# Moving the per-head finish of a cached attention kernel into the next loop turn, and building q and the MLP from wide matmuls

## The chip, the cores and the metric

The kernel runs on one core of one Trainium2 chip. The metric is the device time of one execution in microseconds (us). A run counts as slow if it is over 1.5% above the fastest run of the same kernel, and only fast runs are compared; all timed runs quoted here were fast, except one single look that is marked. "Granted clock" is the share of its full clock that the profile says PE was given in a stretch. The engines are PE (TensorE), VectorE (DVE in the profile), ScalarE (ACT), GpSimd (POOL) and SyncE (SP), which issues almost all DMA.

## The reference

It is one decode step. Attention A: 2 batches, 32 query heads on 8 key/value heads, 32,768 cached positions of width 128. MLP B works on the same input, and the result joins the two.

```python
xn = layernorm(x)                                  # [2,1,512]
q  = (xn @ wq)                                     # 32 heads of 128
p  = softmax(q . k_cache / sqrt(128)); o = p @ v_cache
s  = o.reshape(2, 1, 4096) @ wo
h  = gelu(layernorm(xn) @ w1); ...                 # shifted by 1 or 2 positions: all zero for S = 1
x1 = xn + hs                                       # = xn
g  = silu(x1 + gelu(layernorm(x1) @ w3) @ w4)
out = x + s * g
```

K and V are 134 MB each, so 268 of the 280.5 MB that the kernel reads are cache.

## The kernel before

There are 16 groups (batch, kv head). A group reads 8.4 MB of K and then 8.4 MB of V. All input but x (8 KB, on ScalarE's queue) goes through one SyncE queue in this order: wq, w3, w4, K0, V0, K1, V1, ... K15, V15, wo in eight parts.

```python
# SyncE: what each load waits for
load_k(0)                                # no wait
wait(sp, k_h2); load_v(0)                # the MLP's weights lie in V's buffer
for m in range(1, NG):
    sp.wait_ge(p_k, m); load_k(m)        # first half of group m-1's scores done
    sp.wait_ge(p_o, m); load_v(m)        # group m-1's V products done
for i, (g0, g1, c0, c1) in enumerate(WO_PARTS): ...   # wo parts: 2, 2, 1, 1, 1 kv heads, then 1/2, 1/4, 1/4 of one
```

```python
# PE: prologue (narrow matmuls, weights stationary)
for h in range(Hq):
    for k in range(DK):                  # q: 128 matmuls, 128x2
        pe.matmul(qT_ps[:, h*B:(h+1)*B], lhsT=wq3[:, k, h*Dh:(h+1)*Dh], rhs=xT[:, k, :], ...)
... # up projection 56 matmuls 128x2, down projection 56 matmuls 128x128
with pe.Fori(0, NG):                     # one group
    ... 64 score matmuls, sums, 64 V matmuls
    mm.then_inc(s_o, 1); mark(p_o)
    take(pe, s_ob)                       # the finish: head sums ...
    for t in range(VT): mm = pe.matmul(oT, lhsT=ob[:, t*Dh:(t+1)*Dh], rhs=sel_o[:, t, :], ...)
    mm.then_inc(s_x, 1)
    take(pe, s_on)                       # ... and head rows
    for r in range(NQ): mm = pe.matmul(xp[:, r, :], lhsT=sel_r[:, r, :, :]..., rhs=on[:, :], ...)
    mm.then_inc(s_x, 1)
pe.wait_ge(s_r, NG)                      # all 16 finishes done
for i, (g0, g1, c0, c1) in enumerate(WO_PARTS):
    wait(pe, (d_wo[i], 16)); ...         # 128 wo matmuls in all
```

The finish of a group is what turns its V products into normalized head outputs: ScalarE copies the products (`ob`), PE sums them (head sums) and lays them out (head rows), and VectorE does four short steps between and after. VectorE transposes K for the scores (16 instructions per group), then the exponentials, then its part of the finish (`rec`, `on`, `xm`, `oX`).

The softmax here doesn't subtract the row's maximum and nothing guards it: scores larger than these inputs give would overflow.

## Time and profile before

The time was 655.61 us (median of 3 runs, 655.14 to 656.74). The trace is of a run of 655.52 us, span 654.2 us.

| what | value | read from |
|---|---|---|
| DMA engines busy, rate | 99.2%, 429 GB/s | page |
| PE, VectorE busy | 62%, 52% | page |
| one group, K start to K start | 583.35 - 544.68 = 38.67 us | timeline |
| first V issued / first K block used | 29.58 / 42.53 us | timeline |
| last V half used / wo products / store issued | 641.25 / 648.43 to 651.75 / 652.46 us | timeline |

The page of before: its busy shares (part 1), the DMA row of the 40 slices (part 2), the main queue (part 3), and the chain that ended last (part 4).

```profile
PE 404.3 (62%) x2748; PEld 169.8 (26%) x2748; DVE 337.5 (52%) x429; ACT 71.4 (11%) x167; POOL 5.0 (1%) x18
...
DMA  8999999999999999999999999999999999999997
...
q1 hardware_dynamic: 6748, 280.50, 99.2%
...
PE 1%; DVE 0%; issue 0%; DVEq 0%
```

One resource is busy from end to end and the engines are not. The rate is 429 GB/s over the whole span and 433 from 80 to 649 us (windows view). Whether the engines could move more was not tested.

The timeline of before. The columns are start, duration, engine, line, operation, output and inputs, count, and in brackets the idle time before it with what ended it. First come the prologue's landmarks, then two starts of K transposes a group apart, then the tail.

```profile
18.44 3.57 PE L332 MATMUL bank<-xT,kbuf 128*128 128x2 bf16 x128 [2.09 <-DVE xT L325]
29.58 0.33 SPq L210 DMA_DIRECT2D vbuf<-in_A_v_cache_dram  x1
42.53 18.14 DVE L454 STREAM_TRANSPOSE T<-kbuf 128x1024 int32<-128x1024 int32 x16 [11.90 <-DVEq L46]
...
544.68 18.14 DVE L454 STREAM_TRANSPOSE T<-kbuf 128x1024 int32<-128x1024 int32 x16 [7.83 <-DVEq L46]
583.35 6.88 DVE L454 STREAM_TRANSPOSE T<-kbuf 128x1024 int32<-128x1024 int32 x6 [6.28 <-DVEq L46]
...
641.25 3.48 PE L515 MATMUL bank<-vbuf,pt 128*16 128x512 bf16 x32 [2.44 <-PEq L46]
648.43 3.32 PE L547 MATMUL bank<-kbuf,oX 128*17 128x128 bf16 x128 [0.79 <-DVE oX L472]
651.81 0.29 DVE L555 TENSOR_TENSOR sg<-bank,g 113x128 f32<-113x128 f32 x1 [3.43 <-PE bank L547]
```

VectorE sits idle for 11.9 us before the first K block and for several us in every group. At the end the 128 wo products start only after the last finish (`oX`), and they run in one piece.

### The profile page before, as it was taken

The page shows a single profiled execution, that of the slowest core. Times are in us where ns is not written, and L with a number is a line of the kernel's source. Part 1 is how long each engine was busy: PE and PEld are TensorE (multiplying, and loading weights), DVE is VectorE, ACT ScalarE, POOL GpSimd, SP SyncE. Part 2 cuts the span into 40 slices and gives each one's busy share as a digit, 9 for nine tenths or more (in the row PEclk, how much of TensorE's full clock was granted, in tenths as well). Part 3 has the DMA queues.
Part 4 walks back from the last instruction along what each step waited for, and adds up shares of the span by engine and source line. Part 5 has one row for each costly group of instructions (what it writes and reads, how often), then busy time and mean ns, then how long its engine had stood idle before and what let it go on. Part 6 is the DMA issues. An engine that isn't in the chain of part 4 may idle for free. (4 is left out here: it accounts for less than half of the span.)

```text
span 654.2 us, 7191 instructions
## 1 busy us (share of the span) xinstructions
PE 404.3 (62%) x2748; PEld 169.8 (26%) x2748; DVE 337.5 (52%) x429; ACT 71.4 (11%) x167; POOL 5.0 (1%) x18
## 2 busy tenths in 40 slices
PE   0538394583848558294764819468482956838785
PEld 0513132231323213132331313223131322313323
DVE  3238092653809256290835619074470916538560
ACT  1200102001010201101020010200101020010100
POOL 2000000000000000000000000000000000000000
PEclk9999789685977869697795969877597877869886
DMA  8999999999999999999999999999999999999997
GB/s 369 438 442 445 442 429 421 437 445 445 405 441 441 449 401 449 437 445 421 429 441 441 445 405 445 437 449 409 441 437 445 445 405 441 441 449 393 449 417 298
DMA packets 6766, 280.59 MB, mean 429 GB/s; under 512 B 736, under 2 KB 1000, under 8 KB 2024
## 3 DMA queue, kind: packets, MB, share of 16 engines
q1 hardware_dynamic: 6748, 280.50, 99.2%
q8 instruction: 4, 0.07, 0.0%
q14 instruction: 2, 0.02, 0.0%
q10 hardware_dynamic: 12, 0.01, 0.0%
HBM read 280.50 MB, written 0.00 MB: 429 GB/s over the span
## 5 line engine op out<-in xcount | busy, mean ns | idle before, releaser
L497 PE MATMUL bank<-T,z 128*128 128x512 bf16 x1024 | 282.1, 424 | 168.4 <-PEq L46 163.6
L454 DVE STREAM_TRANSPOSE T<-kbuf 128x1024 int32<-128x1024 int32 x256 | 290.8, 1207 | 129.2 <-DVEq L46 129.1
L497 PEld LDWEIGHTS bank<-T,z 128*128 128x128 bf16 x1024 | 97.5, 103 | 338.9 <-issue 261.6
L515 PE MATMUL bank<-vbuf,pt 128*16 128x512 bf16 x1024 | 77.3, 469 | 2.4 <-PEq L46 2.4
L467 DVE RECIPROCAL rec<-bank 128x4 f32<-128x4 f32 x16 | 2.9, 183 | 124.1 <-DVEq L46 124.1
L433 ACT ACTIVATE ep<-bank 128x512 bf16<-128x512 f32 x32 | 19.1, 597 | 438.2 <-ACTq L46 438.2
L515 PEld LDWEIGHTS bank<-vbuf,pt 128*16 128x16 bf16 x1024 | 28.2, 105 | 43.4 <-issue 28.1
L461 DVE STREAM_TRANSPOSE pt<-ep 128x512 bf16<-128x512 bf16 x32 | 22.1, 691 | 23.4 <-DVEq L46 23.4
L508 PE MATMUL bank<-sm,ones_f 128*128 128x4 f32 x64 | 10.5, 270 | 29.3 <-PEq L46 29.3
L526 PE MATMUL bank<-sel_o,ob 128*128 128x4 f32 x128 | 16.4, 252 | 13.8 <-PEq L46 13.8
L437 ACT COPY ob<-bank 128x512 f32<-128x512 f32 x16 | 9.4, 586 | 109.1 <-ACTq L46 109.1
L426 ACT ACT_TABLE_LOAD x16 | 20.5, 1283 | 0.3
L526 PEld LDWEIGHTS bank<-sel_o,ob 128*128 128x128 f32 x128 | 15.5, 191 | 18.3 <-issue 18.3
L508 PEld LDWEIGHTS bank<-sm,ones_f 128*128 128x128 f32 x64 | 9.6, 215 | 30.2 <-issue 30.2
L426 ACT COPY z<-qr 32x16 bf16 x64 | 12.9, 201 | 0.7
L532 PE MATMUL bank<-on,sel_r 128*128 128x4 bf16 x64 | 3.9, 165 | 12.6 <-PEq L46 12.6
L295 PE MATMUL bank<-ident,xn_bf 17*128 17x17 bf16 x4 | 0.3, 177 | 13.7 <-POOL x L286 13.7
L484 PE MATMUL bank<-ident 128*1 128x1 bf16 x64 | 8.3, 165 | 0.0
L484 PEld LDWEIGHTS bank<-ident 128*1 128x1 bf16 x64 | 4.0, 82 | 16.2 <-issue 14.5
L470 DVE TENSOR_TENSOR xm<-bank,mask 128x16 f32<-128x16 f32 x16 | 2.8, 175 | 8.6 <-DVEq L46 8.6
L532 PEld LDWEIGHTS bank<-on,sel_r 128*128 128x128 bf16 x64 | 2.9, 98 | 13.5 <-issue 13.5
L433 ACT ACTIVATION_READ_ACCUMULATOR ep<-bank 128x1 f32 x32 | 6.3, 198 | 0.2
(67 smaller groups left out, 58.2 us busy)
## 6 DMA issues: line engine op xcount, KB each, us to landing
kbuf<-in_A_k_cache_dram SPq DMA_DIRECT2D x2, 4096.0 KB, 22.1
vbuf<-in_A_v_cache_dram SPq DMA_DIRECT2D x2, 4096.0 KB, 27.2
kbuf<-in_A_wq_dram SPq DMA_DIRECT2D x1, 4096.0 KB, 12.2
vbuf<-in_B_w_dram SPq DMA_DIRECT2D x2, 1792.0 KB, 17.2
kbuf<-in_A_wo_dram SPq DMA_DIRECT2D x2, 1024.0 KB, 34.9
kbuf<-in_A_wo_dram SPq DMA_DIRECT2D x3, 512.0 KB, 37.3
kbuf<-in_A_wo_dram SPq DMA_DIRECT2D x1, 256.0 KB, 26.4
kbuf<-in_A_wo_dram SPq DMA_DIRECT2D x2, 128.0 KB, 15.6
```

The source lines that it names most:

```text
L426: i = act.copy(out=z[32 * j:32 * j + 32, :, :, c:c + rep], in_=qr[32 * j:32 * j + 32, :, :, bass.ds(m * rep, rep)],)
L433: act.activation(out=eps_[i][:, :], in_=sc[i][:, :], func=ACT.Exp, scale=inv_sqrt_dh, accum_out=rss[i][:, :]).then_inc(s_e, 1)
L437: act.copy(out=ob[:, :], in_=o[:, :]).then_inc(s_ob, 1)
L454: dve.transpose(out=Ts[(NR * i + r) % T_BUFS][:, :].rearrange("p (b t k) -> p t b k", b=NB, t=RT), in_=kt[:, r * W:(r + 1) * W].rearrange( ...
L461: dve.transpose(out=pts[h][:, :, :].rearrange("p r (t h) -> p t r h", h=rep), in_=eps_[i][:, :].rearrange("p (t r h) -> p t r h", r=NR, h= ...
L467: then(dve.reciprocal(out=rec[:, :], in_=S))
L484: pe.matmul(mark_ps, lhsT=ident[:, 0:1], rhs=ident[:, 0:1], start=True, stop=True).then_inc(sem, 1)
L497: mm = pe.matmul(sc[i][:, :], lhsT=z[:, nb, e, zc:zc + 128], rhs=Tb[:, nb, :, e], start=(r == 0 and nb == 0 and e == 0), stop=(r == NR - 1 ...
L508: pe.matmul(S, lhsT=ones_f[:, :], rhs=sms[h][:, :], start=(h == 0), stop=(h == NPART - 1))
L515: mm = pe.matmul(o[32 * j:32 * j + VT * rep, :], lhsT=pts[h][:, r, a * VT * rep:(a + 1) * VT * rep], rhs=vt[:, u * VT:(u + 1) * VT, :].rea ...
L526: mm = pe.matmul(oT, lhsT=ob[:, t * Dh:(t + 1) * Dh], rhs=sel_o[:, t, :], start=(t == 0), stop=(t == VT - 1))
L532: mm = pe.matmul(xp[:, r, :], lhsT=sel_r[:, r, :, :].rearrange("p j w -> p (j w)"), rhs=on[:, :], start=True, stop=True,)
```

## The change: intent and diff

The finish of a group moves to the start of the next turn. The last group's finish is left over, and is placed between the wo parts, so that products of heads that are already done need not wait for it. In the prologue, activations become the stationary operand (`lhsT`) and weights the moving one (`rhs`; 128x512 where before has 128x2): 62 wide matmuls on column tiles (each writes 32 of the 128 output partitions, four side by side) replace 240 narrow ones. VectorE transposes put the results back, and ScalarE and GpSimd spread q over the partition groups with 16 copies.

```diff
 # prologue
-    for h in range(Hq):
-        for k in range(DK):
-            i = pe.matmul(qT_ps[:, h * B:(h + 1) * B], lhsT=wq3[:, k, h * Dh:(h + 1) * Dh], rhs=xT[:, k, :], ...)
+    for t in range(NQB):
+        for k in range(DK):
+            for n in range(NQ):
+                i = pe.matmul(sc[t][32 * n:32 * n + 32, :], lhsT=xT[:, k, :],
+                    rhs=wq3[:, k, c:c + GW].rearrange("p (h w e) -> p h e w", h=rep * NB, e=2),
+                    ..., tile_position=(0, 32 * n))
+    for t in range(NQB):
+        k_qT = V(dve.transpose(out=qT[:, :, t * 16:(t + 1) * 16].rearrange("p r k -> p k r"), in_=sc[t]...))
+    for n in range(NQ):
+        for j in range(NQ):
+            if n < 2 or j < 2: k_qa = A(spread(act, j, n))
+            else:              k_qg = G(spread(pool, j, n))
 ... (cut: the two MLP products in the same style; four matmuls that gather the second)
 # loop
 with pe.Fori(0, NG):
+    head_sums()
+    head_rows()
     take(pe, s_z)
 ...
-    take(pe, s_ob) ... head sums ... take(pe, s_on) ... head rows
 # VectorE, in the same way: heads(...) before group(...), once more after the loop
 # tail
-pe.wait_ge(s_r, NG)
-for i, ... in enumerate(WO_PARTS): ...
+pe.wait_ge(s_r, NG)                      # the dummy finish of the first turn makes this "15 groups done"
+product(0)
+head_sums()
+product(1)
+head_rows()
+for i in range(2, len(WO_PARTS)):
+    if WO_PARTS[i][1] == Hkv and WO_PARTS[i - 1][1] < Hkv:
+        pe.wait_ge(s_r, NG + 1)
+    mm = product(i)
```

## The prediction

> **What bounds the kernel now.** The input stream. The page shows the 16 DMA engines 99.2% busy on one queue over the span of 654.2 us: 280.5 MB, 429 GB/s; PE 62%, VectorE 52%. The windows view gives 439 GB/s from 3 to 41 us and 433 from 80 to 649. [...] By the timeline one group takes 38.7 us (K transposes start at 544.7 and 583.4): 16.8 MB at 434 GB/s. Only three places could give time: the queue running dry at the start or in the loop, and the work after the last byte.
>
> **Start.** q, MLP and z setup are done at 32.5 us (timeline), but VectorE gets its first K block only at 42.5. The one load that depends on the prologue, the first V, is issued at 29.6, 12 us before the queue would need it. The change replaces 240 narrow matmuls (q 3.6 us, MLP up 3.5, down 1.7) by 62 wide ones on column tiles, plus 4 fp32 selections. The V products, same 128x512 form on column tiles, run 64 in 3.6 us, so I estimate 2 us for q and under 1 us for each MLP product. VectorE loses about 2 us of selector copies and gains three transposes of 0.5-0.7 us (estimate from 0.69 us for 128x512 bf16). ScalarE gets 12 and GpSimd 4 spreading copies, 0.2-0.3 us each. I expect the first V issue 2 to 4 us earlier, z ready at 27 to 33 us. All of it hides under the K load: worth 0.
>
> **Loop.** The order per engine is the same in a rotated loop: the finish still comes between V products and the next K transposes. The marks that release loads stay. K is issued about 8 us, V about 10 us before the queue runs out. Worth 0.
>
> **End.** The last V half arrives at 641.2; its products end at 644.6, then ob copy, head sums, VectorE, head rows, final oX at 648.4. Only then do 128 wo products run without a wait, 648.43 to 651.79 at a granted clock of 0.5; then two VectorE steps of 0.3 us and the store. But the wo parts are still landing: by issue plus landing time, parts 4 to 7 land at 649.9, 650.5, 650.8 and 651.16. After the change parts 0 to 3 run while PE waited, and behind the last landing only part 7's 4 matmuls remain (26 ns each, plus 0.3 us for one to drain). Their end moves from 651.79 to about 651.5: worth 0.3 us, at most 0.6.
>
> **Prediction: 655.3 us, 654.4 to 656.6.** Faster by over 2%: 0.01; within 2%: 0.98; slower: 0.01.
>
> **What would show it right.** DMA share still 99% at 429-430 GB/s; group period still 38.7 us; first K transpose still at 42.5 us though PE's prologue is shorter; wo products in pieces with PE waiting for landings, the last within 0.2 us of the last landing; the chain of waits ending in a DMA landing rather than the oX reduction.
>
> **What would make it wrong.** The first K transpose or the last landing moving by over 1 us: then the stream depends on something in the prologue that I took to be hidden. Spreading copies or strided and fp32 matmuls so slow that the first V issue passes 42 us would cost the excess.

The sum comes to 655.61 less 0.3 for the end and 0 for start and loop: 655.3 us. Of the terms behind the 0.3 us, 26 ns is 3.35 us / 128, and "0.3 us for one to drain" is the 311 ns that one of these products takes in the trace of before (median; the granted clock was 0.50 up to 651.3 us). The 0.2 to 0.3 us of a spreading copy was an estimate; small copies take 0.21 us on ScalarE (`z`) and 0.28 us on GpSimd (17x128) in that trace.

## The result, and the profile after

The changed kernel takes 655.26 us (median of 6 runs, 655.17 to 655.64), and before in the same comparison 655.21 us (6 runs, 655.12 to 656.74). The ratio is 0.9997, 95% interval 0.9984 to 1.001: the same. (A ratio is the mean time of one kernel's fast runs over that of the other's fast runs of the same rounds, so it is not quite the ratio of the medians quoted.)

The page of after, the same parts as shown of before (its DMA row of the slices is the same, digit for digit):

```profile
PE 403.5 (62%) x2586; PEld 163.9 (25%) x2586; DVE 339.4 (52%) x425; ACT 75.0 (11%) x179; POOL 6.6 (1%) x24
...
q1 hardware_dynamic: 6748, 280.50, 99.3%
...
DMA 4%; SPq 2%; PE 1%; issue 0%; DVE 0%
```

The DMA share is the same, and the chain that ended last now runs back into a DMA rather than into the finish.

The timeline of after, the same landmarks:

```profile
17.35 3.61 PE L347 MATMUL bank<-kbuf,xT 128*32 128x512 bf16 x32 [1.14 <-DVE xT L332]
19.30 1.09 DVE L356 STREAM_TRANSPOSE qT<-bank 128x512 f32<-128x512 f32 x1 [2.00 <-PE bank L347]
22.10 3.86 ACT L363 CAST qr<-qT 32x64 bf16<-32x64 f32 x12 [7.48 <-DVE qT L356]
27.28 0.23 ACT L409 ACTIVATE th<-inner 128x28 f32<-128x28 f32 x1
29.92 0.33 SPq L208 DMA_DIRECT2D vbuf<-in_A_v_cache_dram  x1
...
544.49 18.14 DVE L488 STREAM_TRANSPOSE T<-kbuf 128x1024 int32<-128x1024 int32 x16 [9.30 <-DVEq L46]
583.17 3.50 DVE L488 STREAM_TRANSPOSE T<-kbuf 128x1024 int32<-128x1024 int32 x3 [9.52 <-DVEq L46]
...
641.07 1.90 PE L570 MATMUL bank<-vbuf,pt 128*16 128x512 bf16 x32 [1.53 <-PEq L46]
...
648.44 0.61 PE L590 MATMUL bank<-kbuf,oX 128*17 128x128 bf16 x16 [0.59 <-DMA kbuf<-in_A_wo_dram]
649.69 0.60 PE L590 MATMUL bank<-kbuf,oX 128*17 128x128 bf16 x16 [0.64 <-DMA kbuf<-in_A_wo_dram]
650.48 0.83 PE L590 MATMUL bank<-kbuf,oX 128*17 128x128 bf16 x16 [0.19 <-DMA kbuf<-in_A_wo_dram]
651.37 0.29 DVE L608 TENSOR_TENSOR sg<-bank,g 113x128 f32<-113x128 f32 x1 [3.63 <-PE bank L590]
```

Three readings follow.

- Loop: the period is 583.17 - 544.49 = 38.68 us, against 38.67.
- Start: the first V is issued at 29.92 us, 0.3 us later than before, although far fewer matmuls run. The spreading copies stand in front of `tanh` (`th`) on ScalarE.
- End: the wo products come in six pieces, and five of them wait for a DMA landing (the last three are shown). The last four products start at 651.03 us, 0.04 us after the last landing. The step after them starts at 651.37 instead of 651.81.

Part of those 0.44 us is not the change. The last input packet ends at 650.88 us in the trace of before and at 650.70 in that of after. From that packet to the first packet of the store it takes 2.87 us before and 2.60 us after. So the new end is 0.27 us shorter in this pair of traces, and the rest is where the stream happened to end. The times of before scatter by more than that. And the pair differs in one more thing: the last 32 V products took 3.48 us in before, at a granted clock of 0.53, and 1.90 us in after, at 1.00. The next section sets the 0.27 us against this.

### The profile page after: what moved, and what is told of

Its sections match the earlier page's. It is cut to its first block, busy times and chain, and to the rows that moved or that the text cites. A ratio compares the mean times of both kernels' runs of the same rounds, so it can differ in the third digit from the quotient of the medians.

```text
span 653.8 us, 6890 instructions
## 1 busy us (share of the span) xinstructions
PE 403.5 (62%) x2586; PEld 163.9 (25%) x2586; DVE 339.4 (52%) x425; ACT 75.0 (11%) x179; POOL 6.6 (1%) x24
## 5 line engine op out<-in xcount | busy, mean ns | idle before, releaser
L570 PE MATMUL bank<-vbuf,pt 128*16 128x512 bf16 x1024 | 74.7, 457 | 1.5 <-PEq L46 1.5
L570 PEld LDWEIGHTS bank<-vbuf,pt 128*16 128x16 bf16 x1024 | 28.0, 103 | 40.5 <-issue 23.5
L525 PE MATMUL bank<-sel_o,ob 128*128 128x4 f32 x136 | 18.3, 258 | 14.4 <-PEq L46 14.4
L525 PEld LDWEIGHTS bank<-sel_o,ob 128*128 128x128 f32 x136 | 17.3, 199 | 19.0 <-issue 18.9
L533 PE MATMUL bank<-on,sel_r 128*128 128x4 bf16 x68 | 5.6, 165 | 12.8 <-PEq L46 12.6
```

Of the source, the lines that this page charges most:

```text
L525: mm = pe.matmul(oT, lhsT=ob[:, t * Dh:(t + 1) * Dh], rhs=sel_o[:, t, :], start=(t == 0), stop=(t == VT - 1))
L533: mm = pe.matmul(xp[:, r, :], lhsT=sel_r[:, r, :, :].rearrange("p j w -> p (j w)"), rhs=on[:, :], start=True, stop=True,)
L570: mm = pe.matmul(o[32 * j:32 * j + VT * rep, :], lhsT=pts[h][:, r, a * VT * rep:(a + 1) * VT * rep], rhs=vt[:, u * VT:(u + 1) * VT, :].rea ...
```

## The experiments

The theory is that the input stream sets the time. Then the prologue and the finish are hidden under it, and only work after the last landing (the moment when all data of a load are there) can be saved, which is about 0.3 us. The main rivals are two. First, a gain at the end is real and larger, and the new prologue eats it. Second, the loop is bound by a chain of engines that includes the finish, and the DMA share only follows.

### The two halves alone, and the copies out of the way

`end_only` is the kernel before with the new order of finish and wo. `start_only` is the changed kernel with the old order. `spread_late` is the changed kernel with one block moved:

```diff
 # spread_late: ScalarE and GpSimd copies behind tanh and sigmoid
-    wait(act, k_qT); wait(pool, k_qT); for n ...: for j ...: spread(...)     # in front of the MLP
     ... MLP, tanh, sigmoid ...
+    wait(act, k_qT); wait(pool, k_qT); for n ...: for j ...: spread(...)
```

> The kernel before with only the new order of the finish and the wo parts; prologue untouched. Theory (the input stream binds, and only the work after the last landing can be saved): 0.2 to 0.5 us less than before, wo products in pieces, the last one starting within 0.2 us of the last wo landing, loop period unchanged at 38.7 us. Rival 1 (the finish is on the critical path of the tail for its full length): 4 to 7 us less. Rival 2 (moving the finish in the loop delays K or V issues enough to drain the queue): slower by 1 us or more with a longer group period.

> The changed kernel with the old order of the finish and of wo; only the new prologue differs from before. Theory: within 0.3 us of before, first V issue at about 29.9 us, first K transpose at about 42.4 us, 128 wo products in one block that ends at about 651.8. Rival (the new prologue costs something that cancels a gain at the end): 0.3 us or more slower than before.

> The changed kernel with its 16 spreading copies moved behind tanh and sigmoid on ScalarE's queue. My prediction had the first V issue 2 to 4 us earlier than before, the trace has it 0.3 us later. If the copies in front of tanh (3.9 us on ScalarE) are the reason, the first V issue comes at about 26.4 us, 3 to 4 us earlier than in the changed kernel. If they are not, it stays near 29.9. Time in either case within 0.3 us of the changed kernel (about 655.2), because the first V issue is 12 us ahead of need.

Five runs of each were timed, and before had 655.54 us (9 runs, 655.28 to 656.75).

| kernel | median us (range) | ratio to before (95%) | last input packet to first store packet |
|---|---|---|---|
| end_only | 655.32 (654.89 to 655.53) | 0.9993 (0.9979 to 1.0007) | 2.60 us |
| start_only | 655.44 (655.36 to 656.85) | 1.0000 (0.9986 to 1.0014) | 2.74 us |
| spread_late | 655.25 (654.94 to 655.28) | 0.9991 (0.9977 to 1.0004) | 2.61 us |

No ratio is clear of 1, so the measured times do not prove a gain of 0.3 us. The rival with 4 to 7 us is refuted, and a prologue that eats a gain is not seen (one of a few tenths of a us could not be).

The last column is read from the DMA packets of one trace each. With the new order it is 2.60 or 2.61 in all four traces there are (after, end_only, spread_late and contig, a run below). With the old order it is not fixed: 2.87 and 2.74 here, but 2.60 in act_9, 2.54 in v_less, 3.42 in q_x7 and 4.11 in q_x4, runs of later sections that keep the old end. It goes with the time of the last 32 V products: 1.90 us at a granted clock of 1.00 in act_9 and v_less, 3.1 to 3.6 us at 0.50 to 0.59 in the other four. The tail of act_9 shows the old order with fast V products; the last of its wo products wait for a landing, too:

```profile
643.89 1.90 PE L525 MATMUL bank<-vbuf,pt 128*16 128x512 bf16 x32 [1.81 <-PEq L46]
652.50 1.63 PE L557 MATMUL bank<-kbuf,oX 128*17 128x128 bf16 x32 [0.26 <-DMA kbuf<-in_A_wo_dram]
```

With the new order the last V products took 1.90 us (after, spread_late), 2.95 (end_only) or 3.39 (contig), and the tail stayed the same. So the new end has no fixed worth of 0.27 us. It is worth nothing where the last V products had a granted clock of 1.00 (act_9, v_less), and 0.1 to 0.3 us in the traces of before and start_only (for the longer tails of q_x7 and q_x4 there is no counterpart with the new order). No run set the clock, so this is read across traces and not shown by an experiment. One more observation, not tested: none of the 16 timed runs of after, end_only and spread_late is above 655.64 us, while every list of before (6 to 9 runs) has one to three above 656.3, and start_only has one at 656.85. None of these was traced; a longer tail at the lower clock, as in q_x4, could be the reason.

In spread_late the first V issue moved as it should if the copies delayed it. The timeline of spread_late:

```profile
23.69 0.23 ACT L401 ACTIVATE th<-inner 128x28 f32<-128x28 f32 x1 [7.62 <-DVE inner L399]
25.88 0.33 SPq L208 DMA_DIRECT2D vbuf<-in_A_v_cache_dram  x1
```

It is issued at 25.88 instead of 29.92 us, and the time did not follow. The 12 copies on ScalarE (3.86 us in a row) were the reason for the late issue, together with a load of an activation table (`ACT_TABLE_LOAD`, 1.28 us) that in the changed kernel comes between the last copy and `tanh`; in spread_late it is not on that path.

### Fewer bytes, same compute

```diff
 def load_v(m):                                   # v_less: the kernel before
-    load(A_v_cache, vbuf[:, :], s_v, m)
+    if 0 < m < last:                             # seven eighths of V, the rest keeps old data
+        w = slice(0, 7 * SLOT // 4)
+        sp.dma_start(out=vbuf[:, w], in_=row_view(A_v_cache, *groups[m])[:, w]).then_inc(s_v[0], 16)
+        sp.sem_inc(s_v[1], 16)
+    else:
+        load(A_v_cache, vbuf[:, :], s_v, m)
```

> The kernel before, where groups 1 to 14 load only seven eighths of their V block (the rest keeps older data, so the result is wrong on purpose); all compute stays. 14.7 MB fewer at 433.7 GB/s. Theory (stream binds in the loop): 33 to 34.5 us faster, about 621.4, group period about 36.3 us. Rival (a chain of PE, VectorE and ScalarE binds the loop and the DMA share of 99% only follows it): 0 to 5 us.

It took 621.47 us (4 runs, 621.34 to 621.84) against 655.50, so 34.0 us less, with a group period of 551.90 - 515.64 = 36.26 us:

```profile
515.64 18.14 DVE L459 STREAM_TRANSPOSE T<-kbuf 128x1024 int32<-128x1024 int32 x16 [6.99 <-DVEq L46]
551.90 1.25 DVE L459 STREAM_TRANSPOSE T<-kbuf 128x1024 int32<-128x1024 int32 x1 [5.52 <-DVEq L46]
```

The 14.68 MB left out, at 433 GB/s, are 33.9 us. All instructions of the loop still ran. A group of 15.73 MB in 36.26 us is 434 GB/s, as in before (16.78 MB in 38.67 us). Bytes are what the loop costs. (Its output is wrong, which doesn't matter for the time. The comparison with the reference passed all the same, presumably because attention adds little to this output. It would not notice such an error.)

### How much slack the loop has

Idle copies on ScalarE in front of the second exponential delay the V products, the finish and the next V issue in every group.

```diff
 for i in range(NPART):                           # ScalarE loop of the kernel before
     take(act, s_sc)
+    idle(8 * i)                                  # loop_6;  idle(18 * i) in loop_12
     act.activation(out=eps_[i][:, :], in_=sc[i][:, :], func=ACT.Exp, ...)
+# idle(n): n times act.copy(junk1 <- junk0, 128x512 fp32), each followed by a wait for itself
```

> The kernel before with 8 idle copies (5 to 6.5 us) on ScalarE in every group in front of the second exponential, so that V products, finish and the next V issue come that much later. Read from before: K start to K start takes at least 29.2 us by compute (583.35 to 612.56, where K lay ready) against 38.7 us by the stream, so about 9.5 us of slack. Theory: group period unchanged at 38.7 us, only the last group is exposed at its end by at most a few us, so 0 to 3 us slower in all. Rival (the compute chain with the finish is what sets the period): 5 to 6.5 us per group, 80 to 100 us slower.

> The same with 18 idle copies (11 to 14.5 us per group), more than the slack of 9.5 us. Theory: the queue now runs dry in every group; period 40.5 to 45 us, 30 to 95 us slower, with gaps in the stream. If it is again within 3 us of before, the slack is larger than I read it.

loop_6 took 668.18 us (4 runs, 665.16 to 669.47) and loop_12 took 767.10 us (766.88 to 768.20), against 655.42. The timelines of loop_6 and of loop_12, each with two successive groups:

```profile
546.51 18.14 DVE L464 STREAM_TRANSPOSE T<-kbuf 128x1024 int32<-128x1024 int32 x16 [0.60 <-DVEq L46]
585.17 5.75 DVE L464 STREAM_TRANSPOSE T<-kbuf 128x1024 int32<-128x1024 int32 x5 [1.19 <-DVEq L46]
```

```profile
627.54 18.14 DVE L464 STREAM_TRANSPOSE T<-kbuf 128x1024 int32<-128x1024 int32 x16
672.38 3.50 DVE L464 STREAM_TRANSPOSE T<-kbuf 128x1024 int32<-128x1024 int32 x3 [0.50 <-DVEq L46]
```

With 8 copies (5.7 us) the period stays at 38.66 us: VectorE's idle time before K shrinks from 6 to 8 us to about 1, and the queue stays full. With 18 copies (13.15 us) the period is 44.84 us here, 44.2 to 45.9 in others, and the DMA packets show gaps of 4.3 to 6.5 us in every group. So the slack lies between 5.7 and 13.2 us. I had read 9.5; the delay minus the longer period, 13.15 - 6.2, gives about 7. The finish has room for several us per group in the loop, and shortening it there gains nothing.

My expectation of at most 3 us for loop_6 missed the end. In its profiled run (665.16 us, the fastest of the four; what the median has on top, 3.0 us, was not traced) the stream ends 1.8 us later than before, and 7.8 us more come after the last input packet (10.68 us to the store instead of 2.87). The last group has no next load to hide under. Its delay came out in full, plus the wo products that then had to wait for it. My 30 to 95 us for loop_12 missed in the same way: it was 111.7 us slower. The last input packet came 93.6 us later, but the tail behind it took 21.03 us instead of 2.87.

### Which end of the stream hides the finish

The eight wo parts are queued ahead of the last V block instead of behind it, once in each kernel:

```diff
     sp.wait_ge(p_o, m)
+    if m == last:
+        for i, (g0, g1, c0, c1) in enumerate(WO_PARTS): d_wo[i].after(sp.dma_start(...), 16)
     load_v(m)
-for i, (g0, g1, c0, c1) in enumerate(WO_PARTS): d_wo[i].after(sp.dma_start(...), 16)
```

> The kernel before, with the wo parts queued ahead of the last V block instead of behind it; nothing else changes. Now the stream ends with V, so the last products, the finish and the 128 wo products all lie behind the last landing: read from the trace of before, landing at about 651.0 plus 3.4 products, 3.8 finish, 3.4 wo, in all about 10.6 us, where before has 0.6. Theory (wo landing last is what hides the finish): about 10 us slower than before, 665. Rival (the finish is not hidden by the wo landing): within 2 us of before.

> The changed kernel with the same move of the wo parts. Theory: here the interleaving of finish and wo parts is on the critical path, and is worth 1.5 to 3 us: about 662 to 663.5, against about 665 of the same move on the kernel before. Rival (interleaving has no value of its own): no difference between the two.

The kernel before with this move took 665.95 us (4 runs, 665.28 to 666.98), and the changed kernel with it 662.46 us (662.26 to 662.96). Unmoved, before had 655.76 in the same rounds (655.09 to 656.75). The timelines of the two tails, first of wo_first_before, then of wo_first_after:

```profile
651.41 3.59 PE L516 MATMUL bank<-vbuf,pt 128*16 128x512 bf16 x32 [6.03 <-PEq L46]
659.52 3.60 PE L548 MATMUL bank<-kbuf,oX 128*17 128x128 bf16 x128 [0.79 <-DVE oX L473]
663.17 0.29 DVE L556 TENSOR_TENSOR sg<-bank,g 113x128 f32<-113x128 f32 x1 [3.70 <-PE bank L548]
```

```profile
651.33 3.59 PE L571 MATMUL bank<-vbuf,pt 128*16 128x512 bf16 x32 [6.04 <-PEq L46]
654.71 1.07 PE L591 MATMUL bank<-kbuf,oX 128*17 128x128 bf16 x32
657.00 0.63 PE L591 MATMUL bank<-kbuf,oX 128*17 128x128 bf16 x32
658.02 1.17 PE L591 MATMUL bank<-kbuf,oX 128*17 128x128 bf16 x64
659.24 0.29 DVE L609 TENSOR_TENSOR sg<-bank,g 113x128 f32<-113x128 f32 x1 [0.51 <-PE bank L591]
```

With the tail exposed, the interleaving is worth 665.95 - 662.46 = 3.5 us; I had expected 1.5 to 3. Some of that may be clock: the windows view grants 0.50 during the wo products of the first trace and 0.82 in the second, and the head sums between took 1.84 and 1.28 us. Whether the busier PE brought the clock about is not shown. With wo landing last, the interleaving is worth at most 0.3 us in the traces of before and after. This is where most of the possible gain went: before the change, the landing of wo already hid the finish and most of the wo products.

### How much slack the prologue has

Two kernels repeat the q matmuls of before (the result stays right), and a third delays `tanh` by idle copies:

```diff
-for h in range(Hq):
+for h in list(range(Hq)) * 4:                    # q_x4;  * 7 in q_x7
     for k in range(DK): pe.matmul(qT_ps[:, h*B:(h+1)*B], ...)
 # act_9
+idle(12)                                         # ScalarE, in front of tanh
 k = A(act.activation(out=th[:, :], in_=inner[:, :], func=ACT.Tanh, scale=GELU_C))
```

> The kernel before with its 128 q matmuls done four times (three of them redundant, same result): 3 times 3.5 us more prologue. The first V issue moves from 29.6 to about 40.1 us; the data queued ahead of it end at 41.84. Theory (prologue hidden under the first K load): 0 to 0.5 us slower. Rival (prologue exposed one for one): 10.5 us slower, about 666.

> The kernel before with its q matmuls done seven times: 6 times 3.5 us more, first V issue at about 50.6 us. Theory: the slack of about 12 us is used up and the queue stands empty from 41.8 to about 51.6 us (issue plus 1 us to the first packet), so 9 to 10.5 us slower, about 665. Rival (prologue exposed one for one): 21 us slower, about 676. Rival (prologue never matters): 0.

> The kernel before with 12 idle copies (128x512 fp32, about 0.6 to 0.8 us each with the wait between them) on ScalarE in front of tanh: the first V issue goes from 29.6 to about 37 to 39 us, without more code for PE (the redundant q matmuls of the two earlier runs turned out to stall PE 3.5 us per 128, so those runs overshot the slack). The data queued ahead end at 41.85. Theory (12 us of slack in front of the first V issue): 0 to 0.4 us slower, no gap in the stream. Rival (prologue exposed one for one): 7 to 10 us slower.

The "1 us to the first packet" of q_x7 agrees with the first load in the trace of before: issued at 0.73, first packet at 1.76 us. The 0.6 to 0.8 us of an idle copy was an estimate: one ScalarE copy of 128x512 fp32 takes 0.59 us in that trace, and the twelve with their waits then took 8.72 us in act_9.

| kernel | first V issued at, us | median us (range) | before, same rounds | ratio (95%) |
|---|---|---|---|---|
| act_9 | 39.65 | 658.17 (657.82 to 658.47) | 655.42 | 1.004 (1.0023 to 1.0056) |
| q_x4 | 51.37 | 667.95 (666.09 to 669.98) | 655.50 | 1.0181 (1.0163 to 1.02) |
| q_x7 | 61.55 | 679.19 (677.58 to 679.62) | 655.50 | 1.0354 (1.0337 to 1.0371) |

All three of my expectations failed here, for two reasons. I had expected at most 0.4, 0.5 and 10.5 us more; it was 2.75, 12.45 and 23.69.

The first is the size of the delay. Three more passes of q moved the V issue by 21.8 us, not by 10.5. The timeline of q_x4, PE only, shows why, and one line of q_x7 shows when it stops:

```profile
18.44 5.81 PE L332 MATMUL bank<-xT,kbuf 128*128 128x2 bf16 x212 [2.09 <-DVE xT L325]
28.18 3.55 PE L332 MATMUL bank<-xT,kbuf 128*128 128x2 bf16 x128 [3.93 <-issue]
35.48 3.55 PE L332 MATMUL bank<-xT,kbuf 128*128 128x2 bf16 x128 [3.75 <-issue]
42.50 1.31 PE L332 MATMUL bank<-xT,kbuf 128*128 128x2 bf16 x44 [3.47 <-issue]
```

```profile
42.31 11.68 PE L332 MATMUL bank<-xT,kbuf 128*128 128x2 bf16 x428 [3.20 <-issue]
```

PE pauses for 3.5 to 3.9 us per 128 matmuls, and nothing in the program makes it wait. In the DMA records a packet of 16,384 bytes on the instruction queue starts at 25.76, 33.17 and 40.26 us, and each time PE resumes 2.2 to 2.4 us later. In q_x7 the data queue is empty from 41.85 us; the instruction packets then come every 3.5 us, and 428 matmuls run without a pause. I read this as PE waiting for its instructions (128 matmuls and 128 weight loads per pause) while the data stream kept the DMA engines full. That is inferred from these times; no run tested it.

The second is the slack itself. I had taken 12 us, since the last byte ahead of V0 moves at 41.84 us. act_9 issues V at 39.65, before that moment, and still pays 2.75 us. The view of equal windows, first of before, then of act_9 (the last two columns are DMA share and GB/s):

```profile
36.00:56.00 20.00, 11.96 (x46) 4.31 (x46) 13.47 (x12) 0.80 (x2) 0.00 (x0) 1.00 0.97 420
```

```profile
36.00:56.00 20.00, 13.56 (x101) 5.92 (x102) 14.74 (x17) 5.78 (x11) 0.00 (x0) 1.00 0.91 381
```

act_9 moves (420 - 381) x 20 us = 0.78 MB less in this window, which is 1.8 us at 433 GB/s. With the bytes of each packet spread over its duration, the rate per microsecond from 39 us on is this:

```
act_9   429 172 305 335 349 426   GB/s in 39-40, 40-41, ... 44-45
before  433 433 433 433 435 433
q_x4    433 149  40   0   0   0   (V issued at 51.37: 0 until 52, then 160 341 342 379 433)
```

q_x4 shows that most engines are out of work at about 40.2 us (14 of the last 16 packets of K end at 40.0 to 40.5 us, the other two at 41.66 and 41.84). Both show that the stream needs 4 to 5 us from the V issue to full rate: in q_x4 the first packets come 0.96 us after it (the issuing instruction itself takes 0.33 us), and the first 16 take 2.7 to 3.4 us each, later ones of the same size 2.42. So the issue has to come well before 40.2 us. (The end of the kernel before thins out in the same way: from 397 GB/s in 648.5 to 649.0 us to 113 in 649.5 to 650.0, while packets run to 650.88.) A measure of the slack, worked out from these runs, is how much later V was issued than in before, minus how much later the first 24.6 MB had moved: 10.1 - 1.9 = 8.2 us (act_9), 21.8 - 12.0 = 9.8 (q_x4), 32.0 - 23.2 = 8.8 (q_x7). It is 8 to 10 us, not 12. About 0.9 us of act_9's cost is not in this loss. Its trace shows as much at the other end: the first 280.3 MB are through 1.6 us later than in before, but the last packet comes 2.6 us later, with only about 25 GB/s moving in its last 1.2 us. I do not know why. The rivals of one-for-one exposure fail: 10.1 us of delay cost 2.75. Both kernels, before and after, issue V at 29.6 to 29.9 us and stay clear of the edge.

### Why the wide q matmuls were not faster

```diff
-rhs=wq3[:, k, c:c + GW].rearrange("p (h w e) -> p h e w", h=rep * NB, e=2)
+rhs=wq3[:, k, c:c + GW]                          # contig: contiguous reads
-out=qT[:, :, t * 16:(t + 1) * 16].rearrange("p r k -> p k r")
+out=(the same size, contiguous)                  # contig: contiguous writes of the transposes
```

> The changed kernel, q matmuls reading wq contiguously instead of every second bf16, and the two q transposes writing contiguously instead of with a stride of 32 fp32 (wrong result on purpose). I had estimated 2 us for the 32 wide q matmuls and 0.5 to 0.7 us for a transpose; the trace has 3.6 and 1.08 us. If the strides are the reason: about 2 us, and 0.6 to 0.7 us each. If the wide form or PSUM source is the reason: unchanged.

This was a single look (655.16 us, state unknown), and its result is wrong on purpose. The timeline of contig:

```profile
17.38 3.61 PE L347 MATMUL bank<-kbuf,xT 128*32 128x512 bf16 x32 [1.14 <-DVE xT L332]
19.33 0.72 DVE L356 STREAM_TRANSPOSE qT<-bank 128x512 f32<-128x512 f32 x1 [2.00 <-PE bank L347]
```

The two stride theories part here. The transposes fall from 1.08 to 0.72 us, so the strided write cost 0.36 us each. The matmuls stay at 3.61 us, so their stride costs nothing (at the clock they had; see below). My estimate of 2 us came from V products at a granted clock of 1.00 (64 in 3.63 us). The view of one source line (smallest, median and largest duration in ns) shows the q matmuls of after; the V products of before near 641 us, where the windows view grants 0.53, then those near 605 us, where it grants 1.00; the second MLP product of after, in the same form as q, where it grants 0.50; and the first MLP product in contig:

```profile
L347 PE MATMUL bank<-kbuf,xT x32: 606/628/629, 17.4 to 20.3; 128*32 128x512 bf16 x32
```

```profile
L515 PE MATMUL bank<-vbuf,pt x32: 527/634/634, 641.3 to 644.2; 128*16 128x512 bf16 x32
```

```profile
L515 PE MATMUL bank<-vbuf,pt x60: 379/379/383, 605.2 to 608.2; 128*16 128x512 bf16 x60
```

```profile
L421 PE MATMUL bank<-vbuf,h_bf x14: 607/634/635, 28.0 to 29.2; 128*32 128x512 bf16 x14
```

```profile
L386 PE MATMUL bank<-vbuf,xT x16: 581/581/581, 20.8 to 21.9; 128*32 128x448 bf16 x16
```

The q matmuls (628 ns, median) take as long as V products at a granted clock of 0.53 (634 ns), not 379 ns as at 1.00. The windows view lists a granted clock of 1.00 in this stretch, but that is no evidence: the clock records in the trace of after begin only at 21.6 us (with 1.00), and the view counts time without a record as 1.00. At 21.5 us the matmuls of the first MLP product fall from 581 to about 400 and then 352 ns; in contig, whose records begin at 23.0 us, all 16 take 581. So by its times q ran as at a clock of about 0.5, and my estimate of 2 us used the wrong clock. This is inferred from durations: no clock record covers q, and no run changed the clock on purpose.

## Why the prediction was right, and where it was not

- **Time.** 655.3 us was predicted and 655.26 measured. That it fits to 0.04 us is luck: 655.3 was 655.61 less 0.3, and before had 655.21 in the comparison, so the times show no gain at all. The chain of reasons held: the stream binds (v_less: 34.0 us for 33.9 us worth of bytes), and the loop has slack (loop_6 keeps the period, loop_12 does not).
- **Loop, "worth 0".** Right. The period was 38.68 us against 38.67.
- **End, "worth 0.3 us, at most 0.6".** Right in mechanism: the wo products wait for landings, and exposed, the same interleaving is worth 3.5 us. The size is 0.27 us between the two profiles, but the prediction took the low clock in the tail of its one trace as given. At a granted clock of 1.00 there the old order has nothing left to save (2.60 us from the last input packet to the store in act_9, 2.54 in v_less). That the two profiles differ by about the predicted amount is in part luck. The value in time is below what five rounds resolve.
- **Start, "worth 0".** Right in effect, wrong in its sum. The step "I expect the first V issue 2 to 4 us earlier" failed: it came 0.3 us later (29.92 against 29.58). Mis-sized terms were q (2 us estimated, 3.6 measured), the MLP products (under 1 us each estimated, 1.34 and 1.89 measured; the second took 1.68 before), the q transposes (0.5 to 0.7 us estimated, 1.08 measured, 0.36 of it the strided write), and above all the 12 copies on ScalarE. I had priced them nearly right (0.30 us each), but left them out of the path to V, although they run in front of `tanh`: 3.86 us. spread_late gives 4.0 us back. z was ready at 34.25 us in the trace of after, not at 27 to 33.
- **Start, "12 us before the queue would need it".** Too much. It is 8 to 10 us, because most DMA engines run out before the last one (40.2 against 41.84 us in q_x4) and the stream takes 4 to 5 us from issue to full rate (act_9, q_x4).
- **Signs in the profile.** All came as named, except the landmark of the first V issue. K started at 42.45 us, and the last wo products began 0.04 us after the last landing. The chain that ends in a DMA is a weak sign: act_9, with the old order, has it too.

No version tried that reads all the data is clearly faster than both kernels. spread_late has the lowest median of its rounds, but its interval includes 1.

## What to carry to other kernels

Before shortening a chain at the end of a stream-bound kernel, ask what is still landing meanwhile: the same reordering was worth 3.5 us where the stream had ended and 0 to 0.3 us where small parts were still arriving (0 at a granted clock of 1.00 in the last V products, 0.27 at 0.53, in before). Here the slack of a load had to be counted to the moment when most DMA engines had run out (40.2 us), with 4 to 5 us of lead for the restart, and not to the last byte (41.84 us). When work moves to another engine's queue, add it to everything that stands behind it there (here 3.86 us of copies in front of `tanh`), not only to that engine's busy time.
